# An order planner that models the transfers: one wire, eight in flight, a margin on landings and a limit on how far SP runs ahead

## The chip, the cores and the metric

One core of one Trainium2 chip runs the whole program in one launch. The metric is the device time of the program in microseconds, the median of three runs. A core has TensorE (PE) for matrix products and transposes, VectorE (DVE), ScalarE (ACT) and GpSimd (POOL) for elementwise work, and SyncE (SP), which here only issues DMA transfers. Each engine takes its instructions strictly in the order in which the program lists them for it.

## The reference

Three stages follow one another, with B = 2, H = 8, S = 768, D = 64:

```python
def _attn_ref(q, k, v, proj):                      # (2, 8, 768, 64); proj (64, 6)
    q_bucket, k_bucket = ...                       # 6 sign bits of q @ proj and k @ proj, as a number
    mask = q_bucket[:, :, :, None] == k_bucket[:, :, None, :]
    scores = scale * np.matmul(q, k.transpose(0, 1, 3, 2))
    scores = np.where(mask, scores, -1000000000.0)
    attn = softmax(scores)
    return np.matmul(attn, v)
def _moe_ref(x, w_gate, wq, wk, wv, wo):           # x (2, 768, 512), 4 experts of width 64, 2 chosen
    topk, w = ...                                  # the two best gates of a token, softmax of the two
    for e in range(E):
        q, k, v = x @ wq[e], x @ wk[e], x @ wv[e]
        a = softmax(causal(scale * (q @ k.transpose(0, 2, 1))))
        ye = a @ v @ wo[e]
        out += chosen(e) * w(e) * ye
    return out
def _moe2_ref(x, w_theta, w_tok_r, w_tok_i, w_ch):
    theta = x @ w_theta
    zr, zi = x * np.cos(theta), x * np.sin(theta)
    y = np.einsum('ts,bsd->btd', w_tok_r, zr) + np.einsum('ts,bsd->btd', w_tok_i, zi)
    u = x + y
    return u + np.maximum(u @ w_ch, 0.0)
```

(softmax, causal and chosen stand for the lines that the reference writes out.) Some weights come as 64-bit floats; the program reads them as int64 words and turns them into 32-bit floats itself.

## The kernel before

**The work.** Each float32 operand is split into a high and a low part, and a product is three or four matmuls of these. The attention stage, about the first 290 us, handles pairs of heads: 8 groups of 12 units of 128 rows. A unit has its scores (line 628, into a PSUM tile `ps`), a pass of VectorE that takes the row minimum of the negated scores (line 637, `ss`), the exponential on ScalarE (line 644), six transposes (line 650), a split of the result (lines 661 and 664) and the product with V (line 680, into `O`). ScalarE copies `O` into `ob` (line 694), once for two pairs of units. The MoE projections (lines 827 and 892) and the MoE units with causal scores follow, and then the last stage: `theta` and out projection (line 1070), the token mixing (line 1180) and the channel product (line 1094).

**The transfers.** Nearly all are issued by SyncE. For each later group of the attention stage: the loads of q, k and v (lines 723, 724, 728) into `raw`, a tag of three buffers; and two packs (line 801), one a head, each of six copies of 192 KB inside SBUF (from `sqh`, `sql`, `skh`, `skl` into `op` tiles, 64 partitions of 3072 bytes) and two copies of the hash bits (12 partitions, 36 KB). The scores of a head read what its pack wrote. For the output of a group, `swap` (line 578) copies the half of `ob` that lies on the wrong partitions into `bt`, 192 KB, twice a group; POOL adds the other half (line 582); six transposes spread the softmax denominators into a `ps` tile (line 587); and VectorE multiplies that tile by `bt` into `x` (line 595), which frees the `ps` tile. The three buffers of the tag `ps` are handed out in the order in which the program names the tiles. `load_weights` (line 520) loads one weight block after another into `wraw`, a single buffer that POOL splits (line 527). In the first MoE the projections are put away in DRAM (`qk_d`, lines 905 to 907) and fetched later (line 917). `decode` (lines 443 to 454) and `decode_later` (line 459) load an int64 block of 512 KB, convert it, and store 256 KB in `tok_d` or `wth_d`, which is loaded again where it is used (line 469).

**What sets the order.** The program is written once in program order; tile positions such as `PREP`, `FIN`, `M0F` and `EARLY` say behind which unit a step is named. Then `Plan` reads all instructions with their dependences and makes a new order for each engine. `price` gives each instruction a step (how long it holds its engine) and a time to completion (`late`); `lag` is the wait that a dependence adds. `forward` is a list scheduler: at each point it takes, of the instructions of an engine that can start earliest, the one with the lowest `rank`; buffers and their reuse are kept. `backward` does the same from the end, and gives each instruction the latest time at which it can start without making the plan longer; that is the next rank. `arrange` does six such rounds and keeps the plan whose last TensorE instruction starts first. `fix` makes the chosen order the order of the instruction lists. Only the order reaches the chip: at run time an instruction starts when its engine's earlier ones have issued and its semaphores are there, not at its planned time.

**The prices of a transfer before.** The step on the issuing engine is 620 ns inside SBUF, 440 ns otherwise; the landing comes 2600 ns (inside SBUF) or 2900 ns plus 7 ns a kilobyte after the start, and for the 12-partition copies the pair is 850 and 7500 ns. A consumer waits 50 ns more. Transfers do not delay one another in the plan, and there is no limit on how many are under way.

Of the kernel before, what the change touches and what calls it, by code (L numbers as in the profile page):

```python
# [20 lines left out]
B, H, S, D = 2, 8, 768, 64  # L21
# [38 lines left out]
SIGN = 0x80000000  # L60
REBIAS = 2.0 ** -112
SLACK = 60.0
SPARE = 38


# [34 lines left out]
    return x[0][0] <= y[0][0] and y[0][1] <= x[0][1] and y[1] & ~x[1] == 0  # L100


def price(o):

    n = max([math.prod(c for _, c in x[4]) for x in o.w + o.r if x[1] != "D"] + [1])
    src = [x[1] for x in o.r if x[1] != "D"]
    parts = o.w[0][2][1] - o.w[0][2][0] if o.w else 0
    if o.kind == "InstDMACopy":
        kb = n * parts * 4 >> 10 if o.w[0][1] != "D" else 256
        if o.w[0][1] != "D" and parts == 12:  # L110
            return 850, 7500
        inside = o.r[0][1] == o.w[0][1] == "S"
        return (620 if inside else 440), (2600 if inside else 2900) + kb * 7
    if o.eng == "PE":
        n = math.prod(c for _, c in o.r[1][4])
        n = max(n, math.prod(c for _, c in o.r[0][4]))
        if "is_transpose=True" in o.text or n <= 128:
            return (57 if "bf" in o.dt else 109), 272
        return (118, 282) if n <= 260 else (178, 340) if n <= 384 else (427 if "bf" in o.dt else 230, 392)
    n = math.prod(c for _, c in o.w[0][4]) if o.w else 1  # L120
    if o.eng == "DVE":
        crosses = o.r and o.r[0][2][0] // 32 != o.w[0][2][0] // 32
        if n < 30:
            s = 90 if o.kind != "InstReciprocal" else 138
        elif o.kind == "InstTensorScalarPtr" and src == ["S"]:
            s = 66 + n / 1.92
        else:
            s = 75 + n * 1.036
        if crosses:
            s = max(s, 80 + n * 1.18)  # L130
        if len(o.w) > 1:
            s = 82 + n * 1.045
        return s, s + 80
    if o.eng == "Activation":
        if "Type.Exp" in o.text:
            return 130 + n * 1.042, 130 + n * 1.05
        if "Type.Sin" in o.text or "Type.Abs" in o.text:
            s = 640 if "Type.Abs" in o.text or len(o.r) > 1 else 540
        elif "P" in src:
            s = 45 + n * 0.84 if parts == 128 else 810  # L140
        else:
            s = (571 if "Type.Copy" in o.text else 95 + n * 0.835)
        return s, s + 100
    s = 45 + n * 2.3 if o.kind == "InstTensorTensor" else 165 + n * 0.82
    return s, s + 35
# [50 lines left out]
def lag(a, b):  # L196

    if a.kind == "InstDMACopy":
        return a.late + 50
    if a.eng == b.eng:  # L200
        return a.step
    return a.late + {"PE": 55, "Pool": 85}.get(b.eng, 35)


class Plan:
# [49 lines left out]
        if a != b:  # L255
            self.pre[b][a] = max(self.pre[b].get(a, 0), lag(self.ops[a], self.ops[b]) if ns is None else ns)

    def forward(self, rank, slack=0.0, peek=0.0):


        ops = self.ops
        t = [-1.0] * len(ops)
        missing = [len(p) for p in self.pre]
        ready = [0.0] * len(ops)
        engines = ("PE", "DVE", "Activation", "Pool", "SP")
        free = dict.fromkeys(engines, 0.0)
        heads = {e: [] for e in engines}
        for o in self.todo:
            if not missing[o.n]:
                heads[o.eng].append(o.n)  # L270
        left = {k: len(v) for k, v in self.users.items()}
        slots = {k: [(0.0, "")] * b for k, (b, _) in self.tags.items()}
        turn = dict.fromkeys(self.tags, 0)
        live, reuse = set(), []
        order = {e: [] for e in engines}
        dve = pool = 0.0
        for _ in self.todo:
            best = None
            for e in engines:
                could = []  # L280
                for n in heads[e]:
                    at = max(free[e], ready[n])
                    for name in self.limited[n]:
                        if name in live:
                            continue
                        tag = self.tag[name]
                        if self.tags[tag][1][turn[tag]] != name or not slots[tag]:
                            break
                        old = slots[tag][0][1]
                        if old:  # L290
                            at = max(at, max(t[k] + lag(ops[k], ops[n]) for k in self.leave[old]))
                    else:
                        could.append((at, rank[n], n))
                if could:
                    soon = min(could)[0] + (peek if e == "PE" else 0.0)
                    at, _, n = min((x for x in could if x[0] <= soon), key=lambda x: (x[1], x[0]))
                    if best is None or at < best[0]:
                        best = at, e, n
            assert best, "no instruction can go on"
            at, e, n = best  # L300
            o = ops[n]
            if o.port:
                at = max(at, pool)
                dve = at + o.step
            if e == "Pool":
                at = max(at, dve)
                pool = at + o.step
            t[n], free[e] = at, at + o.step
            heads[e].remove(n)
            order[e].append(n)  # L310
            for name in self.limited[n]:
                tag = self.tag[name]
                if name not in live:
                    live.add(name)
                    turn[tag] += 1
                    old = slots[tag].pop(0)[1]
                    if old:
                        reuse.append((old, name))
                left[name] -= 1
                if not left[name]:  # L320
                    slots[tag].append((max(t[k] + ops[k].late for k in self.leave[name]), name))
                    slots[tag].sort()
            for k, v in self.post[n]:
                missing[k] -= 1
                if ops[k].eng != e and v:
                    v += slack
                if at + v > ready[k]:
                    ready[k] = at + v
                if not missing[k] and ops[k].kind != "BassTilePoolBoundary":
                    heads[ops[k].eng].append(k)  # L330
        return t, order, reuse

    def backward(self, t, reuse, slack=0.0):
# [20 lines left out]
        for _ in self.todo:  # L354
# [9 lines left out]
            last[n] = free[e] = at + ops[n].step  # L364
            heads[e].remove(n)
            for j, v in pre[n].items():
                v += slack if ops[j].eng != e and v else 0
                least[j] = max(least[j], last[n] + v)
                missing[j] -= 1
# [4 lines left out]

    def arrange(self, slack, rounds):

        rank, best = list(range(len(self.ops))), None
        for _ in range(rounds):
            t, order, reuse = self.forward(rank, slack)
            end = max(t[n] for n in order["PE"])  # L380
            if best is None or end < best[0]:
                best = end, t, order, reuse
# [915 lines left out]
```

## Time and profile before

| | |
|---|---|
| median of three runs | 546.54 us |
| the three runs | 542.35, 546.54, 549.32 us |
| the profiled execution: span from the first to the last instruction | 552.3 us |
| mean granted TensorE clock over the span | 0.987 |
| busy: VectorE, ScalarE, POOL | 80%, 67%, 50% of the span |
| moved by the DMA engines | 80.54 MB, 146 GB/s on the mean |
| DMA transfers issued by SyncE, share of 16 DMA engines | 76.50 MB, 51.1% |

The profile gives no other time of the profiled execution than its span, which is longer than each of the three timed runs. A matmul counts as busy from its start to its modelled end, and matmuls overlap, so a busy TensorE can still be short of its peak; but where TensorE is idle, or its clock has fallen, time is open. A granted clock of 1.00 is 2.4 GHz and 0.50 is 1.2 GHz; a value between them is the mean of a stretch that has both. The chain of waits is followed back from the last instruction: what stands in it as a DMA lasted from the issue of that transfer to the moment at which it released the next step.

### The profile page before, as it was taken

What the parts mean: (1) busy time and instruction counts of PE and PEld (TensorE: products, weight loads), DVE (VectorE), ACT (ScalarE), POOL (GpSimd) and SP (SyncE); (2) the same over time, 40 slices, a digit from 0 to 9 for tenths busy, and PEclk for the clock granted to TensorE, in tenths of its full rate; (3) what the DMA queues carried; (4) which work ended last, traced back from release to release, by engine and by line L of the source; (5) the groups of instructions that cost most, each with busy time, mean ns of one, the idle gap of its engine ahead of it and who ended that gap; (6) DMA issues with size and microseconds to landing.
All of it is one profiled execution on the core that took longest, in us unless ns stands there. A gap on an engine that the chain in (4) does not pass through costs nothing.

```text
span 552.3 us, 9725 instructions
## 1 busy us (share of the span) xinstructions
PE 532.0 (96%) x3408; PEld 469.9 (85%) x3408; DVE 441.1 (80%) x721; ACT 369.6 (67%) x675; POOL 277.3 (50%) x233
## 2 busy tenths in 40 slices
PE   8899899999989999889999999998999999999997
PEld 5799799999979999779998998786888888888886
DVE  6798598999977799678989986888987999963343
ACT  4788497988746687648897755898666676563110
POOL 5765969174404555651322121654866778975000
PEclk9999799999989999989999999999999999999999
DMA  7986786556388679958641622343435443241012
GB/s 211 233 189 146 197 208 167 130 118 177 92 257 227 233 180 249 218 176 263 144 121 29 210 77 58 84 128 105 121 108 172 131 142 110 80 133 37 24 66 82
DMA packets 33968, 80.54 MB, mean 146 GB/s; under 512 B 5272, under 2 KB 6808, under 8 KB 33920
## 3 DMA queue, kind: packets, MB, share of 16 engines
q1 hardware_dynamic: 31680, 76.50, 51.1%
q10 hardware_dynamic: 2240, 3.42, 1.7%
q8 instruction: 27, 0.44, 0.3%
q14 instruction: 21, 0.17, 0.1%
HBM read 40.65 MB, written 14.16 MB: 99 GB/s over the span
## 4 chain that ended last, share of the span: by engine, by line
PE 76%; DMA 9%; ACT 5%; DVE 4%; issue 2%; POOL 2%; SPq 1%; ACTq 0%; POOLq 0%
PE yp L1180 18%; PE ps L628 12%; PE O L680 11%; PE ps L650 11%; PE wk L1094 6%; PE ps L892 5%; PE wk L1070 5%; DMA bt<-ob 3%; PE ps L827 3%; ACT ss L644 2%; DMA qk_d<-op 1%; DVE PTl L664 1%; DMA raw<-in_vP_dram 1%; DMA op<-skh 1%; PE ps L776 1%
## 5 line engine op out<-in xcount | busy, mean ns | idle before, releaser
L637 DVE TENSOR_SCALAR_CACHE_REDUCE ss<-ps 128x768 f32<-128x768 f32 (+3 forms) x144 | 118.9, 841 | 27.9 <-PE ps L628 19.7
L661 ACT CAST PTh<-ps 128x768 fp32r<-128x768 f32 x120 | 98.1, 818 | 50.3 <-PE ps L650 49.7
L664 DVE TENSOR_TENSOR PTl<-ps,PTh 128x768 fp32r<-128x768 f32 x120 | 116.6, 979 | 15.7 <-ACT PTh L661 14.7
L644 ACT ACTIVATE ss<-ss,m 128x768 f32<-128x768 f32 (+3 forms) x144 | 122.0, 848 | 9.8 <-DVE ss L637 9.0
L628 PE MATMUL ps<-op 128*128 128x256 f32 (+5 forms) x520 | 118.2, 348 | 8.4 <-DVE x L595 5.4
L650 PE MATMUL ps<-ident,ss 128*128 128x128 f32 x744 | 103.9, 277 | 0.7 <-ACT ss L644 0.5
L680 PE MATMUL O<-PTh,V 128*128 128x256 f32 (+1 forms) x384 | 100.1, 291 | 1.2 <-ACT PTh L661 1.2
L680 PE MATMUL O<-PTl,V 128*128 128x256 f32 (+1 forms) x384 | 99.8, 293 | 0.0
L628 PEld LDWEIGHTS ps<-op 128*128 128x128 f32 (+1 forms) x520 | 80.9, 192 | 15.6 <-DVE x L595 6.2
L650 PEld LDWEIGHTS ps<-ident,ss 128*128 128x128 f32 x744 | 85.2, 142 | 5.7 <-ACT ss L644 1.0
L582 POOL TENSOR_TENSOR bt<-bt,ob 64x768 f32<-64x768 f32 x23 | 42.7, 1856 | 88.7 <-DMA bt<-ob 78.4
L1180 PE MATMUL yp<-zh,tok 128*128 128x512 f32 x264 | 86.4, 394 | 0.0
L680 PEld LDWEIGHTS O<-PTh,V 128*128 128x128 f32 x384 | 74.2, 193 | 2.2 <-ACT PTh L661 1.3
L680 PEld LDWEIGHTS O<-PTl,V 128*128 128x128 f32 x384 | 74.1, 193 | 1.1
L1180 PEld LDWEIGHTS yp<-zh,tok 128*128 128x128 f32 x264 | 49.6, 188 | 10.4
L1180 PE MATMUL yp<-zl,tok 128*128 128x512 f32 x132 | 51.2, 392 | 0.0
L476 POOL TENSOR_TENSOR tok<-raw,tok 128x512 fp32r<-128x512 f32 x27 | 40.9, 1529 | 8.3 <-ACT tok L473 8.1
L572 POOL TENSOR_SCALAR rb<-r 128x768 f32<-128x768 f32 x12 | 10.0, 836 | 61.6 <-DVE r L710 24.9
L1180 PEld LDWEIGHTS yp<-zl,tok 128*128 128x128 f32 x132 | 24.8, 188 | 5.0
L1085 ACT CAST uTh<-wk 128x512 fp32r<-128x512 f32 x12 | 7.1, 588 | 32.7 <-PE wk L1082 28.9
L450 DVE SCALAR_TENSOR_TENSOR g<-raw,g 128x512 uint32<-128x512 uint32 x26 | 28.3, 1088 | 0.7
L1201 DVE SCALAR_TENSOR_TENSOR o<-wk,x 128x512 f32<-128x512 f32 (+1 forms) x13 | 8.4, 649 | 25.0 <-PE wk L1094 24.9
(199 smaller groups left out, 1015.6 us busy)
## 6 DMA issues: line engine op xcount, KB each, us to landing
raw<-in_wtok_dram SPq DMA_DIRECT2D x18, 512.0 KB
raw<-tok_d SPq DMA_DIRECT2D x27, 256.0 KB
op<-sqh SPq DMA_DIRECT2D x30, 192.0 KB
op<-skh SPq DMA_DIRECT2D x30, 192.0 KB
bt<-ob SPq DMA_DIRECT2D x24, 192.0 KB
tok_d<-g SPq DMA_DIRECT2D x18, 256.0 KB
raw<-in_vP_dram SPq DMA_DIRECT2D x8, 384.0 KB
op<-qk_d SPq DMA_DIRECT2D x16, 192.0 KB
```

The source lines that it names most:

```text
L450: nc.vector.scalar_tensor_tensor(gu, words[:, :, 0], 29, gu, op0=OP.logical_shift_right, op1=OP.bitwise_or)
L476: nc.gpsimd.tensor_sub(l, raw, f(h))
L582: engine.tensor_add(self.bt[keep], self.bt[keep], self.ob[keep, side])
L628: nc.tensor.matmul(self.sp[:, c0:c1], lhs, rhs[:, c0 - off:c1 - off], start=a == 0, stop=last)
L637: nc.vector.tensor_scalar(self.ss[:, off:off + w], self.sp[:, off:off + w], -0.125, NEG, op0=OP.mult, op1=OP.min, accum_out=m)
L644: nc.scalar.activation(self.P[:, off:off + w], self.ss[:, off:off + w], AF.Exp, bias=m, scale=-1.0, accum_out=self.grp.den[:, side, i:i + 1])
L650: nc.tensor.transpose(self.pt[:, j * 128:(j + 1) * 128], self.P[:, j * 128:(j + 1) * 128], ident)
L661: nc.scalar.copy(self.d[0], self.v)
L664: nc.vector.tensor_sub(self.d[1], self.v, f(self.d[0]))
L680: nc.tensor.matmul(o, g.V[:, j, side, :], rhs, start=j == 0 and a == 0, stop=j == w // 128 - 1 and a == 1)
L1094: nc.tensor.matmul(o, lhs[:, sl], rhs[:, kd, cols], start=n == 0, stop=n == 3 * NK - 1)
L1180: nc.tensor.matmul(yp[t], lhs[:, a, t, :], rhs[:, a], start=i == 0 and a == 0 and n == 0, stop=i == NT - 1 and a == 1 and n == 2)
```

## The change

The planner gets a model of the transfers. `transfer` gives the time on the wire: bytes of one of 16 queues by a rate for source and target (load 25, store 21, inside SBUF 12.5 bytes a nanosecond), times 1.1. `price` takes this for all DMAs, with a lead of 2300 ns and steps of 400, 570 and 800 ns. In `forward` one wire serves all transfers in turn; a transfer's landing is where the wire is free of it, and this is written into `late`. A transfer cannot start before the eighth one back has landed. `lag` adds 1000 ns to every landing. From the second round on a transfer on SP is planned no earlier than 24 us before its rank. `forward` and `backward` take the lag of a DMA anew, since its landing is now known only in the plan. No tile, no instruction of the computation and no position changes.

```diff
@@ -60,6 +60,11 @@
 SIGN = 0x80000000
 REBIAS = 2.0 ** -112
 SLACK = 60.0
+DMA_LEAD = 2300.0
+DMA_WORSE = 1.1
+DMA_LANES = 8
+DMA_MARGIN = 1000.0
+HOLD = 24e3
 SPARE = 38
 
 
@@ -100,17 +105,23 @@
     return x[0][0] <= y[0][0] and y[0][1] <= x[0][1] and y[1] & ~x[1] == 0
 
 
+def transfer(o):
+
+    x = o.w[0] if o.w[0][1] != "D" else o.r[0]
+    rate = {"DS": 25.0, "SD": 21.0, "SS": 12.5}[o.r[0][1] + o.w[0][1]]
+    wide = 4 * math.prod(c for _, c in x[4])
+    return math.ceil((x[2][1] - x[2][0]) / 16) * wide / rate * DMA_WORSE
+
+
 def price(o):
 
     n = max([math.prod(c for _, c in x[4]) for x in o.w + o.r if x[1] != "D"] + [1])
     src = [x[1] for x in o.r if x[1] != "D"]
     parts = o.w[0][2][1] - o.w[0][2][0] if o.w else 0
     if o.kind == "InstDMACopy":
-        kb = n * parts * 4 >> 10 if o.w[0][1] != "D" else 256
-        if o.w[0][1] != "D" and parts == 12:
-            return 850, 7500
+        o.move = transfer(o)
         inside = o.r[0][1] == o.w[0][1] == "S"
-        return (620 if inside else 440), (2600 if inside else 2900) + kb * 7
+        return (800 if parts == 12 else 570 if inside else 400), DMA_LEAD + o.move
     if o.eng == "PE":
         n = math.prod(c for _, c in o.r[1][4])
         n = max(n, math.prod(c for _, c in o.r[0][4]))
@@ -196,7 +207,7 @@
 def lag(a, b):
 
     if a.kind == "InstDMACopy":
-        return a.late + 50
+        return a.late + 50 + DMA_MARGIN
     if a.eng == b.eng:
         return a.step
     return a.late + {"PE": 55, "Pool": 85}.get(b.eng, 35)
@@ -255,7 +266,7 @@
         if a != b:
             self.pre[b][a] = max(self.pre[b].get(a, 0), lag(self.ops[a], self.ops[b]) if ns is None else ns)
 
-    def forward(self, rank, slack=0.0, peek=0.0):
+    def forward(self, rank, slack=0.0, peek=0.0, hold=None):
 
 
         ops = self.ops
@@ -273,13 +284,19 @@
         turn = dict.fromkeys(self.tags, 0)
         live, reuse = set(), []
         order = {e: [] for e in engines}
-        dve = pool = 0.0
+        dve = pool = wire = 0.0
+        lanes = []
         for _ in self.todo:
             best = None
             for e in engines:
                 could = []
                 for n in heads[e]:
                     at = max(free[e], ready[n])
+                    if ops[n].kind == "InstDMACopy":
+                        if len(lanes) >= DMA_LANES:
+                            at = max(at, lanes[-DMA_LANES])
+                        if hold and e == "SP":
+                            at = max(at, rank[n] - hold)
                     for name in self.limited[n]:
                         if name in live:
                             continue
@@ -306,6 +323,10 @@
                 at = max(at, dve)
                 pool = at + o.step
             t[n], free[e] = at, at + o.step
+            if o.kind == "InstDMACopy":
+                wire = max(wire, at + DMA_LEAD) + o.move
+                o.late = wire - at
+                lanes.append(wire)
             heads[e].remove(n)
             order[e].append(n)
             for name in self.limited[n]:
@@ -322,6 +343,8 @@
                     slots[tag].sort()
             for k, v in self.post[n]:
                 missing[k] -= 1
+                if o.kind == "InstDMACopy" and v:
+                    v = lag(o, ops[k])
                 if ops[k].eng != e and v:
                     v += slack
                 if at + v > ready[k]:
@@ -364,6 +387,8 @@
             last[n] = free[e] = at + ops[n].step
             heads[e].remove(n)
             for j, v in pre[n].items():
+                if ops[j].kind == "InstDMACopy" and v:
+                    v = lag(ops[j], ops[n])
                 v += slack if ops[j].eng != e and v else 0
                 least[j] = max(least[j], last[n] + v)
                 missing[j] -= 1
@@ -374,9 +399,10 @@
 
     def arrange(self, slack, rounds):
 
-        rank, best = list(range(len(self.ops))), None
+        rank, best, hold = list(range(len(self.ops))), None, None
         for _ in range(rounds):
-            t, order, reuse = self.forward(rank, slack)
+            t, order, reuse = self.forward(rank, slack, hold=hold)
+            hold = HOLD
             end = max(t[n] for n in order["PE"])
             if best is None or end < best[0]:
                 best = end, t, order, reuse
```

## Rows read from the trace of the kernel before

**Rows 1.** The page: busy time by engine, and the granted clock in 40 slices.

```profile
PE 532.0 (96%) x3408; PEld 469.9 (85%) x3408; DVE 441.1 (80%) x721; ACT 369.6 (67%) x675; POOL 277.3 (50%) x233
...
PEclk9999799999989999989999999999999999999999
```

**Rows 2.** Windows by stage: length, engines' busy us, clock, DMA share, GB/s.

```profile
0.00:290.00 290.00, 277.06 (x1991) 253.78 (x1992) 242.13 (x429) 213.81 (x380) 151.53 (x149) 0.98 0.71 187
290.00:345.00 55.00, 54.89 (x410) 49.87 (x409) 45.92 (x104) 36.87 (x80) 10.54 (x8) 1.00 0.33 94
345.00:385.00 40.00, 35.97 (x260) 31.11 (x259) 33.60 (x62) 35.62 (x70) 22.09 (x18) 1.00 0.37 104
385.00:510.00 125.00, 125.00 (x555) 102.54 (x554) 103.88 (x104) 78.56 (x137) 93.09 (x59) 1.00 0.37 116
```

**Rows 3.** Windows, the same columns, around three places in the attention stage.

```profile
56.00:68.00 12.00, 9.37 (x52) 8.70 (x51) 6.22 (x10) 4.97 (x10) 10.78 (x10) 0.72 0.79 192
160.00:168.00 8.00, 5.91 (x32) 5.44 (x32) 5.79 (x9) 2.82 (x6) 0.00 (x0) 0.79 0.85 256
224.00:228.00 4.00, 3.16 (x19) 2.38 (x18) 2.62 (x5) 3.35 (x6) 2.31 (x4) 1.00 1.05 209
232.00:244.00 12.00, 9.24 (x60) 8.61 (x58) 6.87 (x11) 5.97 (x11) 8.34 (x8) 0.86 0.51 139
```

**Rows 4.** Waits, 0 to 290 us: total us, times, longest us.

```profile
PE ps L628 <- DVE x L595: 5.4, 2, 2.8
PE ps L628 <- DVE op L903: 2.1, 1, 2.1
...
POOL bt L582 <- DMA bt<-ob: 37.3, 9, 8.9
...
SPq L520 <- DMA wraw<-in_wvg_dram: 8.3, 2, 6.6
```

**Rows 5.** Chain that ended last, in order of time: start us, us, what.

```profile
54.49 3.50 DMA bt<-ob
...
153.13 8.15 DMA qk_d<-op
...
212.01 7.15 DMA raw<-in_vP_dram
219.19 6.92 DMA op<-skh
226.17 7.70 DMA bt<-ob
```

**Rows 6.** SyncE's timeline, 36 to 64 us: start us, us, what it issues.

```profile
45.73 0.33 SPq L520 DMA_DIRECT2D wraw<-in_wvg_dram  x1
54.05 0.33 SPq L520 DMA_DIRECT2D wraw<-in_wqk_dram  x1
```

**Rows 7.** SyncE's timeline, 140 to 170 us.

```profile
152.60 0.44 SPq L459 DMA_DIRECT2D raw<-in_wtok_dram  x1
```

**Rows 8.** SyncE's timeline, 210 to 240 us.

```profile
212.44 0.42 SPq L453 DMA_DIRECT2D tok_d<-g  x1
...
224.84 0.33 SPq L469 DMA_DIRECT2D raw<-wth_d  x1
225.21 0.46 SPq L801 DMA_DIRECT2D op<-sql  x1
```

**Rows 9.** ScalarE's timeline, 44 to 62 us and 205 to 240 us.

```profile
47.42 0.58 ACT L694 COPY ob<-O 128x512 f32<-128x512 f32 x1
...
223.30 0.60 ACT L694 COPY ob<-O 128x512 f32<-128x512 f32 x1
```

**Rows 10.** DMA issues by line: times issued, KB each.

```profile
raw<-in_wtok_dram SPq DMA_DIRECT2D x18, 512.0 KB
...
op<-bits SPq DMA_DIRECT2D x30, 36.0 KB
```

## The prediction

> **What bounds the kernel now.** First the page's busy times and slices [rows 1]: TensorE is busy for 532.0 of 552.3 us, so 20.3 us of idle time are open, and the granted clock is full but for three slices in the middle. Then the stages [rows 2]. From 290 to 345 us and from 385 to 510 us TensorE is busy throughout (54.89 of 55 and 125.00 of 125), with the DMA engines 0.33 and 0.37 busy: no transfer can save time there. From 345 to 385 us 4.0 us are idle, again with the DMA engines only 0.37 busy. Transfers can matter in the attention stage, 0 to 290 us: 12.9 us idle, DMA engines 0.71 busy on the mean.
>
> There the idle time is lumped [rows 3]. Stop 1, from 58 us: 12.00 - 9.37 = 2.63 us idle. Stop 2, at 160 us: 2.09. Stop 3, at 234 us: 2.76, and 0.84 before it, at 226 us. Behind each of the three the granted clock falls from 2.4 towards 1.2 GHz, and these are the three slices of rows 1. The missing share of the clock is work not done while TensorE is busy: 0.28 x 12 = 3.4 us at stop 1, 0.21 x 8 = 1.7 at stop 2, 0.14 x 12 = 1.7 at stop 3. So the stops cost 6.0, 3.8 and 4.4 + 0.8 = 5.3 us, **15.1 us in all, 2.7% of the span**. A better order of transfers can reach about that; the other 4.6 us of this stage are small or lie at the start.
>
> The waits of TensorE say what it waited for [rows 4]: VectorE's x (5.4 us in two waits) and op (2.1 us), both of which read PSUM tiles. The scores need one of three such tiles, whose order the program fixes, and a finish step holds one until bt has come. So the planner cannot put the holder behind the scores; it can only bring the transfer earlier. In the chain of waits a DMA is last in all three stops [rows 5], and one kind of transfer, bt<-ob of 192 KB, takes 3.50 us from issue to landing at 54 us and 7.70 us at 226 us.
>
> **The change part by part.** No instruction on an engine is added or removed; prices, and through them the order on each queue, change.
>
> *Landing.* The old price of a 192 KB copy inside SBUF is 2600 + 192 x 7 = 3944 ns whatever else is on its way: right at 54 us, half of the truth at 226 us. The new one is 2300 + 4 x 3072 / 12.5 x 1.1 = 2300 + 1081 ns, and it queues behind all that is on the wire. Tested on the trace: between the landing of raw<-in_vP (212.01 + 7.15 = 219.16) and that of bt<-ob (226.17 + 7.70 = 233.87) [rows 5] lie 16 transfers, those issued from 212.44 to 226.17, the first and the one before the last in [rows 8]. Twelve are copies inside SBUF (12 x 1.081), one a 256 KB store (0.858), two 256 KB loads (0.721 each), one a 128 KB load (0.360): 15.6 us by the new prices, 14.7 in the trace. So the serial wire is right within 6% where it matters.
>
> Here a page speaks against it. The Trainium skill, "DMA: Bandwidth & Descriptors", section "Anatomy of one DMA", gives a fixed 2.0 us and then 436 bytes a nanosecond, whatever source and target; an estimate by it is 0.45 us of movement for 192 KB. By that the plan would space copies inside SBUF more than twice too far, stop 3 would not come of a full wire, and only stop 1 would be won. The trace disagrees: 14.7 us for those 16.
>
> *Eight in flight.* The chain steps from the vP issued at 212.01 to the skh issued at 219.19, when vP had landed, and on to the bt issued at 226.17, when skh had landed [rows 5]; eight issues lie between. So the limit is there already, and the plan now knows it: no cost.
>
> *Int64 loads.* They are 512 KB [rows 10], but the price counts four bytes an element: 8 x 2048 / 25 x 1.1 = 0.72 us, half of what the same formula gives for their bytes. Such a load leaves just before the transfer of stop 2 [rows 7].
>
> *SP's issue steps* go from 620 to 570, 440 to 400 and 850 to 800 ns; the rows have 0.33 to 0.46 us [rows 6, 8], and the old order waited on data and landings, not on issue. Taken at nothing: an error of 50 ns is covered by those waits, and without them eight issues would come 0.4 us later or sooner in a step of 7 us.
>
> **Stop 1.** The copy into ob ends at 47.42 + 0.58 = 48.0 us [rows 9], but its bt<-ob is issued at 54.49 [rows 5]. SyncE stands before the wqk load of 54.05 [rows 6], which may not overwrite wraw until POOL has split the wvg weights, and that split waits for a load issued at 45.73 which the old price lands after 2900 + 130 x 7 = 3.8 us. The wire was full, and SyncE waited up to 6.6 us for it [rows 4]. With the queue on the wire counted, the wqk load belongs behind bt<-ob. Then bt<-ob leaves at 48 us and lands after 3.50 to 7.70 us, at 51.5 to 55.7 instead of 58.0; 2.3 us is the least gain, so of the gap of 2.63 us 0.3 is the most that stays. POOL's add then comes ahead of weight splits, whose results are wanted only when the projections begin. Gain 2.63 + 3.4 = **6.0 us**; bounds 0 (the order stays) and 6.0.
>
> **Stop 3.** ob is ready at 223.30 + 0.60 = 223.9 [rows 9], bt<-ob issued at 226.17, behind a load and an sql of the next pack [rows 8]. In front of those it leaves 2.3 us earlier, and on the same full wire lands 2.3 us earlier; 0.5 us of the gap is left, too short for the clock to fall if 226 us is a guide (0.84 idle, clock 1.00 [rows 3]). Gain 2.3 + 1.7 = **4.0 us**; bounds 0 and 5.3. The sql put behind lands about 1.1 us later, its new price; that pack still lacks its bits by then, so it is covered; without the cover the 1.1 us would come off the gain.
>
> **Stop 2.** VectorE's op waits for the stash of X, which left at 153.13 but took 8.15 us [rows 5] on a wire with int64 loads. The hold to 24 us before need can move a load out of its way; the halved price of these loads argues that the plan still sees too free a wire. Between 0 and 3.8 us, I take half: **1.9 us**.
>
> **What the new order adds.** The trace of before has no row for it. A new stop of stop 2's size costs 3.8 us, the nearest price; none and four are the bounds. I take one: lists change on all five queues, and this is the cheapest of the three stops seen.
>
> The hold and the margin of 1 us on landings delay planned work and act on the chip through order alone. A rule speaks against the hold: the Trainium skill, the same page, "Rules for kernel authors", says to issue a DMA early and wait for it late. By it every load put back is a risk, and the time would be that of the third case below. The rows set 24 us against a longest landing of 8.15: three times as much, so no cost in the sum.
>
> Sum: 6.0 + 4.0 + 1.9 - 3.8 = 8.1 us off. The profiled span, 552.3, is 5.8 above the median of the three runs (546.5) and above the highest (549.3); that execution may have had a little more of the stops. I take 8.1 off the median: **538.4 us**.
>
> **Rivals.**
> - All three stops go and nothing new comes: 546.5 - 15.1 = 531.4 us. For it: one cause, a full wire that the old prices don't see, stands behind all three. Against it: stop 2's transfer already left early, and the wire stays as full. Chance 0.24.
> - The stops only move: what bt<-ob gains, a pack, a stash or a held load loses, as the full wire hands the lateness on; or the order hardly changes. 544 to 549, say 546 us. For it: DMA engines 0.71 busy in the stage, 1.05 before stop 3 [rows 2, 3]. Chance 0.26. The page's faster copies, at 0.02 of this, would give 6.0 - 3.8 = 2.2 us, so 544.3.
> - Slower: the bits. Their 36 KB copies, 30 in 15 pairs [rows 10], were planned to land at 7.5 us, now at 2300 + 270 + 1050 = 3.6 us on a free wire. Issued last in their pack with so little in hand, they come late to the scores (L628), each time as a stop of 3.8 us. TensorE has no such wait now [rows 4]. Three of 15 pairs eat the 11.9 us of gain, and it decides there; six give 546.5 + 6 x 3.8 - 11.9 = 557.4 us. Against it: wire and margin are counted. Chance 0.10.
> - The forecast: 0.40, from 531 to 544.
>
> **Numbers.** The three runs are 1.3% apart, so about 2% (10.9 us: below 535.6, above 557.5) can be told from no change. Faster by that: nearly all of the first rival (0.22), a third of the forecast (0.14), a little of the second (0.02): 0.38. Slower: half of the bits' case (0.05) and as much for what I have not seen in five new lists, 0.06: 0.11. Within: 0.51. The range runs from the first rival less half the runs' spread (531.4 - 3.5, rounded to 527) to the second's upper end plus 2 (551); it leaves out the bits and the tails, under 0.2. The forecast's own is 531 to 544.
>
> **What would show it.** Right: no fallen clock at 56 to 68 and 232 to 244 us, bt<-ob ahead of the wqk load on SyncE, TensorE's waits for VectorE's x near nothing, POOL's wait for bt<-ob well under its 37.3 us in this stage [rows 4]. Wrong: waits of L628 for op<-bits or op<-skl, a fallen clock at other places, or TensorE idle in the stages after 290 us, where I count no change.

## The result, and the profile after

Changed: **540.76 us** (median of 18 runs, 538.90 to 541.34). Before, in the same comparison: 544.76 us (median of 18 runs, 542.12 to 549.32). The ratio is 0.9912 with an interval of 0.9888 to 0.9936, so 3.5 to 6.1 us off; the medians lie 4.0 us apart. Under 2%, so by the bound of the prediction no difference, but a real one: the interval does not reach 1. The forecast was 538.4 us, a gain of 8.1 us.

The page of the profiled execution of the changed kernel (540.91 us, span 539.1), with the rows that answer to [rows 1]:

```profile
PE 526.0 (98%) x3408; PEld 464.4 (86%) x3408; DVE 446.1 (83%) x721; ACT 368.6 (68%) x675; POOL 277.7 (52%) x233
...
PEclk9999999999999999999999999999999999999999
```

TensorE has as many instructions as before and is busy for 526.0 of 539.1 us: 13.1 us open, where it was 20.3. No slice has a lower clock any more, and the same matmuls take 6.0 us less; the prediction counted 6.8 us of missing clock (3.4, 1.7 and 1.7). Windows of the changed kernel, by stage as in [rows 2] and then around the places of [rows 3] (length, busy us of PE, PEld, DVE, ACT and POOL, clock, DMA share, GB/s):

```profile
0.00:290.00 290.00, 285.42 (x2092) 260.95 (x2093) 253.68 (x449) 223.60 (x404) 156.48 (x152) 1.00 0.72 186
...
385.00:510.00 125.00, 125.00 (x564) 102.83 (x562) 98.33 (x101) 73.28 (x128) 83.40 (x54) 1.00 0.36 106
56.00:68.00 12.00, 11.78 (x92) 10.98 (x91) 11.24 (x20) 9.88 (x18) 11.45 (x11) 1.00 0.62 153
146.00:162.00 16.00, 15.39 (x113) 14.35 (x112) 15.24 (x28) 11.30 (x20) 0.00 (x0) 1.00 0.92 264
212.00:224.00 12.00, 12.00 (x88) 11.02 (x86) 9.87 (x16) 8.55 (x16) 11.57 (x13) 1.00 1.01 216
224.00:236.00 12.00, 12.00 (x90) 11.17 (x90) 11.18 (x19) 9.25 (x19) 5.07 (x6) 1.00 0.53 128
```

All three stops are gone: at the first 0.22 us is idle where 2.63 was, at the second 0.61, at the third nothing in 24 us, and the clock is 1.00 in each. The DMA engines are as full as before (0.72 of the stage, 1.01 ahead of the third place): the same transfers, in another order. Waits of the changed kernel, 0 to 290 us, for [rows 4] (us, times, longest); line numbers are those of before plus 26:

```profile
PE ps L558 <- DVE warm L562: 1.3, 1, 1.3
PE ps L676 <- DVE r L736: 0.9, 2, 0.7
PE ps L676 <- DVE PTl L690: 0.6, 1, 0.6
...
POOL bt L608 <- DMA bt<-ob: 15.1, 4, 6.2
```

TensorE's longest wait in this stage is now 1.3 us, at the very start. None for x is left, and none for bits. POOL waits 15.1 us for bt<-ob, not 37.3. SyncE's timeline, for [rows 5, 6, 8]:

```profile
42.32 0.60 SPq L546 DMA_DIRECT2D wraw<-in_wvg_dram  x1
...
47.88 0.47 SPq L604 DMA_DIRECT2D bt<-ob  x1
...
53.07 0.84 SPq L546 DMA_DIRECT2D wraw<-in_wqk_dram  x1
...
213.06 0.55 SPq L604 DMA_DIRECT2D bt<-ob  x1
```

The bt<-ob of stop 1 leaves at 47.88 us (forecast: 48), ahead of the wqk load, as the prediction had it. That of stop 3 leaves at 213.06, with no fallen clock after it; its ob is ready at 213.02, so it goes at once, where it left 2.3 us late before.

**The profiled execution of before was an unusual one.** Each result lists the granted clock of every run. Over the span of 552.3 us of [rows 1] it was 0.987. The experiments below ran in three comparisons, with 93 runs of before; none has a clock under 0.990. The table has 83 of them: ten slow runs, each over 1.5% above the fastest of its comparison, are left out, so it lacks the longest, and five of those ten have a clock of 0.990 or 0.991.

```
granted clock          runs of before   median us     runs of after   median us
0.999 or 1.000         29               542.58        18              540.76
0.996 or 0.997         37               545.04         0
0.993 or 0.994         17               546.42         0
```

A stop like the third costs 0.14 x 12 = 1.7 us of clock, 0.003 of the span; so one such stop is 0.997, two, or one like the first, 0.994, and three 0.991. By this count the kernel before has no fallen clock in a third of its runs, mostly one stop, sometimes two, and three in 5 of 93. The changed kernel had none in 18 of 18. The 83 together have a median of 544.83 us, all 93 one of 545.04. Of the gain of 4.0 us some 2.2 (544.8 to 542.6) therefore goes with the fallen clock, and 1.8 (542.6 to 540.8) is there without any. This split is rough, as it sets runs of different chips side by side. No run of before at full clock was profiled, so what makes the 1.8 us is not shown; waits for the same transfers, too short to cost clock, are one candidate.

### The profile page after: what moved, and what is told of

It is laid out like the page before. It is cut to its first block, busy times and chain, and to the rows that moved or that the text cites. A ratio compares the mean times of both kernels' runs of the same rounds, so it can differ in the third digit from the quotient of the medians.

```text
span 539.1 us, 9722 instructions
## 1 busy us (share of the span) xinstructions
PE 526.0 (98%) x3408; PEld 464.4 (86%) x3408; DVE 446.1 (83%) x721; ACT 368.6 (68%) x675; POOL 277.7 (52%) x233
## 4 chain that ended last, share of the span: by engine, by line
PE 83%; DVE 9%; ACT 3%; DMA 2%; issue 2%; ACTq 0%; POOL 0%; SPq 0%; DVEq 0%
PE yp L1206 17%; PE ps L654 14%; PE O L706 13%; PE ps L676 13%; PE ps L918 6%; PE wk L1120 6%; PE wk L1096 4%; PE ps L853 3%; DVE PTl L690 2%; DVE ss L663 2%; PE ps L802 2%; PE ps L613 1%; DMA raw<-in_kT_dram 1%; PE wk L1108 1%; DMA wth_d<-g 1%
## 5 line engine op out<-in xcount | busy, mean ns | idle before, releaser
L654 PE MATMUL ps<-op 128*128 128x256 f32 (+5 forms) x520 | 116.9, 344 | 1.1 <-DVE PTl L690 1.0
L676 PE MATMUL ps<-ident,ss 128*128 128x128 f32 x744 | 102.0, 273 | 2.5 <-DVE r L736 0.9
L706 PE MATMUL O<-PTh,V 128*128 128x256 f32 (+1 forms) x384 | 98.3, 289 | 0.5 <-ACT PTh L687 0.5
L706 PE MATMUL O<-PTl,V 128*128 128x256 f32 (+1 forms) x384 | 96.7, 287 | 0.0
L676 PEld LDWEIGHTS ps<-ident,ss 128*128 128x128 f32 x744 | 83.6, 140 | 9.1 <-ACT PTh L687 1.8
L654 PEld LDWEIGHTS ps<-op 128*128 128x128 f32 (+1 forms) x520 | 79.8, 190 | 7.8 <-DVE PTl L690 1.7
L706 PEld LDWEIGHTS O<-PTh,V 128*128 128x128 f32 x384 | 72.6, 189 | 1.6 <-ACT PTh L687 0.6
L706 PEld LDWEIGHTS O<-PTl,V 128*128 128x128 f32 x384 | 72.6, 189 | 0.7
L502 POOL TENSOR_TENSOR tok<-raw,tok 128x512 fp32r<-128x512 f32 x27 | 42.3, 1574 | 10.7 <-ACT tok L499 10.4
L670 ACT ACTIVATION_READ_ACCUMULATOR ss<-ss,m 128x1 f32 x144 | 27.5, 191 | 0.0
```

The source lines that it names most:

```text
L502: nc.gpsimd.tensor_sub(l, raw, f(h))
L654: nc.tensor.matmul(self.sp[:, c0:c1], lhs, rhs[:, c0 - off:c1 - off], start=a == 0, stop=last)
L670: nc.scalar.activation(self.P[:, off:off + w], self.ss[:, off:off + w], AF.Exp, bias=m, scale=-1.0, accum_out=self.grp.den[:, side, i:i + 1])
L676: nc.tensor.transpose(self.pt[:, j * 128:(j + 1) * 128], self.P[:, j * 128:(j + 1) * 128], ident)
L706: nc.tensor.matmul(o, g.V[:, j, side, :], rhs, start=j == 0 and a == 0, stop=j == w // 128 - 1 and a == 1)
```

## The experiments

Each ran in five rounds beside the kernel before on the same chip; a ratio is against that. In the order edits a number is an instruction of SyncE's list.

**Before, unchanged.** To see an ordinary execution. No edit.

> The kernel before once more, unchanged, for a second profile and to see its runs beside each other. Theory: its stops are left to chance from run to run (which transfer lands first, where the clock looks), and the profiled run of before had all three. Then this profile has a span near the timed runs, 541 to 548 us, a granted clock above 0.987, and one or two of the three stops; the time is that of before within 0.3%. Rival: the three stops are fixed by the order. Then the span is again 551 to 554 us with the clock down behind 58, 160 and 234 us.

545.53 us, ratio 1.0007 (0.9980 to 1.0033), span 543.2. Windows of this execution:

```profile
40.00:64.00 24.00, 24.00 (x187) 22.62 (x186) 21.44 (x35) 20.12 (x37) 19.89 (x20) 1.00 0.71 185
140.00:160.00 20.00, 19.76 (x137) 18.07 (x136) 18.52 (x32) 13.25 (x24) 2.16 (x1) 1.00 0.77 238
222.00:234.00 12.00, 9.57 (x62) 8.83 (x61) 6.76 (x11) 6.32 (x12) 8.34 (x8) 0.86 0.61 155
```

Stops 1 and 2 are not there; stop 3 is, with 2.43 us idle and 0.14 x 12 = 1.7 of clock: 4.1 us. Why stop 1 is missing shows on SyncE, in the same order as before:

```profile
42.95 0.40 SPq L520 DMA_DIRECT2D wraw<-in_wvg_dram  x1
...
48.96 0.33 SPq L520 DMA_DIRECT2D wraw<-in_wqk_dram  x1
49.40 0.47 SPq L578 DMA_DIRECT2D bt<-ob  x1
```

From the wvg load to the wqk load go 6.0 us here and 8.3 in [rows 6]; SyncE's wait for that load was 4.3 us here and 6.6 there. The list puts the same bt<-ob behind the same load. It leaves 2.6 us after its ob is ready here (46.77 us on ScalarE) and 6.5 us after it there; 2.3 of these 3.9 us are the longer wait for that one load, and TensorE stops in the one and not in the other. The two executions also test the price of the stops: stops 1 and 2, 6.0 + 3.8 = 9.8 us by the prediction's sum, are in the first alone, and its span is 9.1 us longer.

**One transfer moved in the changed kernel.** bt<-ob of stop 1 goes back behind the six copies and the wqk load:

```diff
+        order = plan.busy(*plan.arrange(SLACK, 6)[:2], 20e3)
+        sp = order["SP"]
+        sp.remove(468)
+        sp.insert(sp.index(615) + 1, 468)
-        plan.fix(tc, plan.busy(*plan.arrange(SLACK, 6)[:2], 20e3))
+        plan.fix(tc, order)
```

> The changed kernel, with one transfer on SyncE moved back: the bt<-ob of stop 1 stands behind six copies of the pack and the wqk load, nine places later than in the changed order, as it stood behind that load before. Theory (a late bt<-ob is a stop of TensorE and may cost the clock): it leaves at about 53.5 instead of 47.9 us, lands at 56 to 58, POOL's add ends at 58 to 60, and the scores that start at 58.2 us wait 1 to 3 us for VectorE's x, with 1.7 to 3.4 us more where the clock falls: 542 to 546 us. Rival (TensorE has other work there and makes the time up by the end of the stage): 540 to 541.5 us.

546.72 us, ratio 1.0051 (1.0024 to 1.0078): the whole gain and more is lost, and the clock is down in 12 of 12 runs. Timeline and window of this kernel:

```profile
53.00 0.90 SPq L604 DMA_DIRECT2D bt<-ob  x1
...
61.47 1.65 PE L654 MATMUL ps<-op 128*128 128x512 f32 x4 [3.88 <-DVE x L621]
```

```profile
56.00:68.00 12.00, 8.12 (x43) 7.53 (x43) 5.09 (x9) 4.17 (x8) 9.13 (x8) 0.72 0.32 82
```

bt<-ob leaves 5.1 us later; TensorE waits 3.88 us for x, then loses 0.28 x 12 = 3.4 us of clock. The span is 5.9 us longer, so some 1.3 of these 7.2 us are made up later. The time is a little above what was expected (542 to 546). This is stop 1 of [rows 3], made by one transfer.

**Before with SyncE's list mended by hand.** bt<-ob of stop 1 ahead of the wqk load, two int64 loads behind the stash, bt<-ob of stop 3 ahead of the load and the sql; then the same with a wo load one copy earlier, (2232, 2339):

```diff
+        for what, behind in ((468, 729), (1508, 1553), (1656, 1611), (2276, 2452)):
+            sp.remove(what)
+            sp.insert(sp.index(behind) + 1, what)
```

> The order of before on all engines; on SyncE alone four transfers are moved: the bt<-ob of stop 1 ahead of the wqk load, the bt<-ob of stop 3 ahead of a load and an sql, and at stop 2 two int64 loads behind the stash. Theory (the gain is the place of these transfers on SyncE): about 541 us, ratio 0.990 to 0.994, clock 1.00 behind all three places. Rival (the gain is spread over the new order of all queues, and the stops are not what sets the median): ratio 0.997 to 1.001.

> The four moves on SyncE that gave 0.9958, and a fifth: the woT load whose split TensorE waited 1.9 us for at 216 us goes one copy forward in the pack. Theory (SyncE's order alone can give the whole gain; that wait and the clock behind it, 2 + 1.7 us, are what was missing): 540.5 to 542 us, ratio 0.990 to 0.994, clock 1.00 in the middle. Rival (on the full wire the stop only moves to the next transfer): 543 to 545 us, another stop between 200 and 260 us.

The first: 543.89 us, ratio 0.9958 (0.9931 to 0.9984), six of 12 runs at full clock. The second: 544.20 us, 0.9993 (0.9957 to 1.0029), three of 12. Waits and a window of the first:

```profile
PE ps L1026 <- POOL wf L428: 1.9, 1, 1.9
```

```profile
214.00:226.00 12.00, 10.00 (x56) 8.47 (x55) 6.50 (x10) 5.56 (x10) 8.40 (x11) 0.86 0.87 206
```

The stop has moved: TensorE now waits for a weight split. That wait was 0.6 us in the ordinary execution. The woT load of the split keeps its place in the list (issued at 210.74 us, there at 211.09), but the split starts 0.6 us later (217.97 against 217.38), and TensorE comes 0.7 us earlier. In the second, with that load earlier, it is x again, at 223 us:

```profile
PE ps L628 <- DVE x L595: 3.1, 1, 3.1
```

Here bt<-ob has left at 215.68 us. But POOL's list, which no hand edit touched, puts the add behind the split of a wth load that left after it, at 216.40. These are POOL's lines in the second edit, and then, around the same add, in the changed kernel:

```profile
223.09 0.62 POOL L428 TENSOR_SCALAR wf<-raw 128x512 fp32r<-128x512 f32 x1 [3.48 <-ACT ob L694]
223.79 1.80 POOL L582 TENSOR_TENSOR bt<-bt,ob 64x768 f32<-64x768 f32 x1
```

```profile
219.60 1.83 POOL L608 TENSOR_TENSOR bt<-bt,ob 64x768 f32<-64x768 f32 x1
...
222.49 0.62 POOL L454 TENSOR_SCALAR wf<-raw 128x512 fp32r<-128x512 f32 x1
```

In the second edit the add starts as soon as the split has ended; the change puts it ahead of the split. So, as far as these lines show, stop 3 takes two lists, SyncE's and POOL's, and the hand edits mended one. The first edit keeps about half of the gain by its ratio, the second has none that is clear of noise: neither theory came out in full, and the rival "the stops only move" describes the traces of both. One number speaks for the theory of the second: its three runs at full clock took 540.27, 540.77 and 540.93 us, as long as the change. Three runs are few, but where no stop comes, five moves on SyncE alone reach the time of the new plan.

**Parts of the change left out or put in alone.** No shared wire; no hold; no margin; no limit of eight; and the old prices with the hold alone:

```diff
-                wire = max(wire, at + DMA_LEAD) + o.move      # a_nowire
+                wire = at + DMA_LEAD + o.move
-            hold = HOLD                                       # a_nohold
+            hold = None
-DMA_MARGIN = 1000.0                                           # a_nomargin
+DMA_MARGIN = 0.0
-DMA_LANES = 8                                                 # a_nolanes
+DMA_LANES = 1000
+                    if hold and e == "SP" and ops[n].kind == "InstDMACopy":   # b_hold
+                        at = max(at, rank[n] - hold)
...
+            hold = 24e3
```

> The changed planner without the shared wire: each transfer lands 2300 ns plus its own movement after its start, whatever else is under way; lanes, margin and hold stay. Theory (knowing the queue on the wire is what puts bt<-ob ahead of the weight load): 544 to 546 us, with at least one of the stops back. Rival (the wire is not needed, the margin of 1 us or the hold does it): 540 to 541.5 us.

> The changed planner without the limit of 24 us on how far SyncE runs ahead. Theory (the hold costs and gives nothing, since eight in flight already limit SyncE): 540 to 541.5 us. Rival (the hold is what keeps early loads from standing before bt<-ob and the stash): 543 to 546 us, with a stop at 160 or 234 us.

> The changed planner with no margin of 1 us on landings. Theory (wire, lanes and hold order the queues; the margin only covers what the wire's price misses): 540 to 542 us, perhaps with a wider spread from run to run. Rival (the margin is what keeps consumers from standing at landings that come late): 543 to 547 us, with waits of TensorE, VectorE or POOL for transfers.

> The changed planner with no limit of eight in flight in the plan (on the chip it stays). Theory (the wire's queue already tells the plan when SyncE is stopped, so the limit adds little): 540 to 542 us. Rival (without it the plan issues whole packs at once, and an urgent transfer stands behind them): 543 to 547 us, with a stop at 215 to 255 us, where the wire is full.

> The planner of before with its old prices and only the hold of 24 us added. Theory (hold and wire are both needed: each alone left out brought a stop back): 543.5 to 547 us, ratio 0.997 to 1.004, with the stop near 225 us. Rival (the hold alone does it, by taking early loads off the full wire): 540 to 541.5 us with no stop.

**Int64 loads at their bytes, and the planner's SLACK at other values.** Both keep the whole model and only make it land on another order (SLACK is 60 in the change):

```diff
-    wide = 4 * math.prod(c for _, c in x[4])                  # a_int64
+    wide = (8 if o.dt.endswith('int64') else 4) * math.prod(c for _, c in x[4])
-SLACK = 60.0                                                  # a_slack50, a_slack40
+SLACK = 50.0                                                  # 40.0
```

> The changed planner with the movement of the int64 loads priced by their bytes (1.44 us instead of 0.72). Theory (a truer wire orders at least as well): 539.5 to 541.5 us. Rival (what counts is which of many near-equal orders the rounds fall on, and any edit of the prices draws anew): anywhere from 541 to 547 us, with a stop at another place.

> The changed planner with another constant that has nothing to do with transfers (50 instead of 60 ns on each dependence between engines), to see how far orders of the same model lie apart. Theory (the model takes the big stops away, and small waits that differ from order to order make the rest): no stop over 1.5 us with a fallen clock before 290 us, time 541 to 545 us. Rival (the measured order is good for its model alone): 540 to 541.5 us.

> As the other, with 40 ns: a second order of the same model. Theory: again no stop with a fallen clock before 290 us, and 541 to 545 us. Rival: 540 to 541.5 us. A stop with a fallen clock here would say that the model does not take them away by itself.

All of these together, with the runs at full clock (0.999 or more) counted:

```
                         median us   ratio (interval)             full clock   median of those
the change               540.76      0.9912 (0.9888 to 0.9936)    18 of 18     540.76
no shared wire           552.02      1.0122 (1.0086 to 1.0158)     0 of 6
old prices, hold alone   553.50      1.0166 (1.0120 to 1.0211)     0 of 6
no hold                  544.98      0.9992 (0.9971 to 1.0013)    11 of 12     544.96
no margin                545.31      1.0012 (0.9987 to 1.0038)    11 of 12     545.26
no limit of eight        543.49      0.9975 (0.9951 to 0.9999)    12 of 12     543.49
int64 at eight bytes     543.48      0.9968 (0.9945 to 0.9990)    10 of 12     543.21
SLACK 50                 545.18      1.0005 (0.9978 to 1.0031)     5 of 12     543.26
SLACK 40                 546.92      1.0046 (1.0019 to 1.0073)    12 of 12     546.92
```

The theories that a part costs nothing when it is left out (the hold, the margin, the limit of eight), and that the true bytes of the int64 loads order at least as well, did not come out: the times lie where their rivals had them, but most runs keep a full clock, without the stops that the rivals named. Without the wire and with the hold alone the times are 6.0 and 6.5 us above the upper end of what was expected; those of SLACK 50 and SLACK 40 are 0.2 and 1.9 us above it.

Two things come apart here. **In these plans the clock goes with the shared wire.** Neither of the two new plans without it keeps a full clock in any run: the hold on old prices, and all the rest of the new ones. These are their windows, without the wire and then with the hold alone:

```profile
224.00:240.00 16.00, 12.60 (x84) 11.78 (x83) 9.59 (x17) 8.86 (x15) 9.01 (x9) 0.89 0.41 104
```

```profile
140.00:152.00 12.00, 8.80 (x47) 7.64 (x46) 7.15 (x11) 4.08 (x9) 5.89 (x4) 0.86 0.23 50
224.00:240.00 16.00, 12.90 (x78) 11.35 (x77) 9.71 (x15) 8.27 (x14) 12.28 (x15) 0.89 0.58 118
```

Each has 3.1 to 3.4 us idle with a fallen clock behind it. Without the wire this is the third place, and its bt<-ob leaves 8.2 us after its ob is ready (216.43 us), behind copies of the next pack:

```profile
224.65 0.60 SPq L604 DMA_DIRECT2D bt<-ob  x1
```

The stop costs 3.4 + 0.11 x 16 = 5.2 us of the 11.3 us by which this plan is above the change; the rest is in smaller waits. Stop 1 needs no wire to go: in both plans without it the bt<-ob of stop 1 leaves as soon as its ob is ready (47.23 after 47.20 us; 46.91 after 46.89), and TensorE is busy throughout from 40 to 80 us. Nor does a late transfer always make a stop: at the third place SLACK 40 issues it 2.7 us after its ob, with a full clock. With the wire, six of seven plans keep the clock in at least 10 of 12 runs. This is strong evidence, but not proof: it sets seven plans against two, and each plan is one draw of an order. The seventh, SLACK 50, has its stop in another stage, at 370 us, where the projection of wk waits for ScalarE's rT (its waits, and its window by stage):

```profile
PE wk L1096 <- ACT rT L616: 2.2, 1, 2.2
```

```profile
345.00:385.00 40.00, 36.27 (x220) 30.87 (x219) 33.94 (x56) 32.75 (x66) 23.16 (x18) 0.96 0.40 119
```

**The rest goes with the order that comes out.** At a full clock the plans with the wire lie between 540.8 and 546.9 us, and the kernel before, when its clock stays up, at 542.6, inside that spread. Against before as it runs, three of the seven are faster clear of noise (the change, no limit of eight, int64 at eight bytes), one is slower (SLACK 40), and three cannot be told from it. So the model brings the full clock, and the 4.0 us only together with the order that the change happened on. SLACK 40 shows where. First the change, then SLACK 40: the matmuls that mask the causal scores (line 656), and those of the mixing stage (line 1206), with duration in ns, first and last start.

```profile
L656 PE MATMUL ps<-upper,identb x48: 219/230/233, 258.9 to 353.7; 128*128 128x128 bf16 x48
...
L1206 PE MATMUL yp<-zh,tok x264: 387/389/496, 383.4 to 523.5; 128*128 128x512 f32 x132
```

```profile
L656 PE MATMUL ps<-upper,identb x48: 219/230/235, 258.9 to 354.6; 128*128 128x128 bf16 x48
...
L1206 PE MATMUL yp<-zh,tok x264: 387/389/504, 383.5 to 528.0; 128*128 128x512 f32 x132
```

Both reach the causal scores at 258.9 us. Then as many mixing matmuls of the same length, from the same time on, end 4.5 us later. SLACK 40 in the window in which the change has 125.00 busy us of 125, and TensorE's waits there:

```profile
385.00:510.00 125.00, 122.48 (x542) 98.47 (x541) 91.53 (x98) 70.63 (x125) 81.28 (x55) 1.00 0.37 110
```

```profile
PE wk L1108 <- DVE rr L1130: 1.2, 1, 1.2
PE yp L1206 <- POOL tok L502: 0.9, 2, 0.6
```

Waits of 0.6 to 1.2 us, after which the clock stayed full, where the change has none. No kernel tried beat the change.

## Why the prediction was right, and where its size was off

**What bounds the kernel: right.** Idle lumps with a fallen clock in the attention stage, each behind a late transfer that holds a PSUM tile. One transfer moved makes such a stop, and the clock is down in 12 of 12 runs.

**Landing: right for stop 3, not shown for stop 1.** Without the shared wire a stop is back at the third place, the clock is down in six of six runs, and the time is 11.3 us above the change. Stop 1 goes without the wire as well, so that "with the queue on the wire counted" is not what moved its transfer. The fit of the Trainium skill, "DMA: Bandwidth & Descriptors", "Anatomy of one DMA", by which stop 3 would have stayed, stands there for transfers that GpSimd issues; SyncE issues the transfers here, and no run times one that GpSimd issues, so the 14.7 us of the trace do not contradict that section. The *eight in flight* at no cost: 543.49 us without the limit, so it is worth up to 2.7 us as it fell out here, by order alone. *Int64 loads* at half their bytes did no harm; the true bytes gave 543.48.

**Stop 1: mechanism right, size only of that execution.** bt<-ob left at 47.88 us and the gap fell to 0.22. The term was 6.0 us; the one moved transfer gives it back as 5.9 us of span. But the ordinary execution of before that was profiled does not have this stop.

**Stop 3: right in size, with a condition overlooked.** Term 4.0 us, in the ordinary execution 4.1, all of it gone. By the timed runs it is less: those with the clock of one stop are 2.5 us longer than those at full clock (545.04 and 542.58). And the working moved the transfer alone, with POOL's add following it. POOL's timeline of before has a weight split just ahead of that add:

```profile
232.03 0.62 POOL L428 TENSOR_SCALAR wf<-raw 128x512 fp32r<-128x512 f32 x1 [1.37 <-DMA raw<-wth_d]
234.03 1.80 POOL L582 TENSOR_TENSOR bt<-bt,ob 64x768 f32<-64x768 f32 x1 [1.39 <-DMA bt<-ob]
```

The add waits 1.39 us for the transfer, so 2.3 us earlier on SyncE alone would have brought at most 1.4; the rest needs the add ahead of that split, where the plan put it.

**Stop 2: mis-sized.** Term 1.9 us; it is gone in the change, but was not in the ordinary execution either. Which part of the model took it away was not tested.

**What the new order adds: not there.** The term of one new stop, 3.8 us against the gain, has nothing in the trace of after. Other orders show that it was no empty fear: SLACK 50 gets such a stop, and the hand edits get one each.

**The step that failed** is the last of the sum: "I take 8.1 off the median". The profiled execution stood 5.8 us above the median, and the text allowed that it "may have had a little more of the stops"; it had all three, where a timed run of before has about one on the mean (71 stops in the 83 runs of the table). Its terms belonged to 552.3, not to 546.5: between the two profiled spans the gain is 13.2 us, between those of the ordinary execution and of after 543.2 - 539.1 = 4.1. Both errors were large and of opposite sign: stops 1 and 2 counted at 7.9 us that the ordinary execution does not have, and 3.8 us of a new stop that did not come. 8.1 - 7.9 + 3.8 = 4.0, which is what was measured. The forecast came nearer to the measured time than its gain to the measured gain (2.4 us off, where the gain was 4.1 off), because the median of three runs that it started from lay 1.8 us above that of the 18: luck. Part of the agreement at 4.0 us is chance too: by the runs at full clock 1.8 of the 4.0 us has nothing to do with fallen clocks, and no term stood for it.

**The rivals.** "All three go and nothing new comes" describes the trace best; its 531.4 us fell to the same step, 15.1 us taken off a run that held some 4. "The stops only move" is what the profiled executions of the hand edits show. "The bits" did not come: TensorE has no wait for them. The warning against the hold, from the Trainium skill, "DMA: Bandwidth & Descriptors", "Rules for kernel authors" (issue the DMA early, wait late), is not borne out in the change: without the hold the runs at full clock are 4.2 us longer (544.96), and TensorE has no wait for a load that was put back. On the old prices it is: the hold alone makes the kernel 8.7 us longer than before (553.50 against 544.84).

**Stages after 290 us: right.** From the first causal scores to the first mixing matmul, and on to the last, the ordinary execution of before and that of after differ by 0.1 and 0.3 us (113.2 and 113.1; 151.2 and 151.5); the gain is made before, with the first causal scores at 258.9 us and not at 263.2.

**Open:** what in the prices makes the mixing stage 1 to 4 us longer in the near-equal plans, where the 1.8 us at full clock come from, and whether the change's order is more than the best draw among them. Seven orders are too few to tell, and the profile of the kernel without the hold is the one of its 12 runs with a stop, so it does not show its ordinary loss.

## What to carry to other kernels

Before a sum is taken off a median, compare the profiled execution's span and granted clock with those of the timed runs; where they differ, profile the same kernel again and weigh each stop by the share of runs that have it. An order that only just makes it can show as a spread of the times (542 to 549 us before, 538.9 to 541.3 after); but SLACK 40, at full clock in every run, spreads from 545.0 to 550.1, so a full clock does not promise steadiness. When a transfer is moved by hand, look at the list of the engine that takes what it brings: here POOL's. And try a planner's model at neighbouring settings: what holds in nearly all of them (here the full clock, in six of seven) is likely the model's, the rest is the order it happened on.

## What was not expected of the hardware

- The same program, with the same order on each queue, stops or not from run to run: of the 83 runs of before in the table, 29 kept a full clock and 17 lost the worth of two stops, 542.6 against 546.4 us.
- One copy of 192 KB that leaves 5.1 us late cost 5.9 us of span, more than its lateness: 3.88 us of waiting, and the clock behind it.
- The length of a wait does not tell by itself whether the clock falls. Waits of TensorE of 1.9 to 3.9 us were followed by a fallen clock wherever they appear above, but one of 1.9 us in the int64 plan was not: in its window 2.08 us are idle and the clock is 1.00. Single waits of up to 1.2 us, as in the mixing stage of SLACK 40, left it full in 12 of 12 runs.

```profile
360.00:370.00 10.00, 7.92 (x52) 6.61 (x51) 9.03 (x10) 8.70 (x16) 6.91 (x5) 1.00 0.09 12
```
